# Fourier mixing and an MLP on one core: a two-element copy moved to VectorE, loads of x and y reordered, y steps placed behind the turning of u

## The chip, the cores and the metric

The kernel runs on one core of a Trainium2 chip. The metric is device time in microseconds, the median of several executions. TensorE multiplies, ScalarE, VectorE and GpSimd work elementwise, and SyncE's queue (SP in the profile) issues almost all DMAs, in order.

## The reference

Eight sequences of 3136 tokens by 256 channels in float32. Each is filtered along the tokens in the frequency domain, then mixed by a two-dimensional FFT of which the real part is added, normalized along the channels, and sent through a two-layer MLP with a ReLU and a residual:

```python
X = np.fft.rfft(x, axis=1)
y = np.fft.irfft(X * (filt_r + 1j * filt_i)[None], n=3136, axis=1).astype(np.float32)
mixed = np.real(np.fft.fft(np.fft.fft(y, axis=1), axis=2))
u = y + mixed
un = (u - u.mean(-1, keepdims=True)) / np.sqrt(u.var(-1, keepdims=True) + 1e-06)
out = u + np.maximum(un @ w_ch1, 0.0) @ w_ch2
```

## The kernel before

The transforms are matmuls with tables, in two steps each way. For every batch `forward1` and `forward2` go from x to the spectrum, multiply by the filter, keep what the mixing needs (`eo`, from `fold_sums` and `fold_halves`) and make the first inverse step, whose result goes to a DRAM scratch `d2`. `inverse2` reads pieces of `d2` (tile `b2`, 512 KB for batch 0), makes the second inverse step and writes y to DRAM (`dy`). Both are generators: `advance(n)` runs the forward one up to step n, `give(n)` the inverse one up to step n.

Tokens then go in groups of 256 pairs. A group needs its mixing (`mixture`), y read back from `dy` (`fetch`), the normalization and two products of the MLP: `first_product(g, f)` for eight slices f of the hidden channels, and `second_product(g, f)`. In the main loop `q = 8 g + f`.

Group 0 is special. Its y does not go through DRAM: `direct()` in `inverse2` sums it on TensorE into two PSUM tiles (`sums`), from near tiles and a table, in place of steps 0 and 1 of `inverse2`. `prepare_first` copies the mixing to `near` and `point` on ScalarE, spreads it to y on VectorE (lines 1078 to 1080) and GpSimd (line 1083), copies two Nyquist elements of one row (line 1086, ScalarE), adds the sums (line 1091), takes moments (1040, 1041), the root (1046, ScalarE) and five small scales (1052 to 1056, VectorE), forms u in two halves (1103, 1110, 1112) and turns it by 16 transposes on TensorE (line 327, `flip`), copied out by ScalarE and VectorE. Only then can `first_product(0, 0)` begin.

Batch 0's step c of `inverse2` for c from 2 is one matmul over half a piece (line 903), a copy by ScalarE (909) and, after every second one, four stores to `dy` (826). Piece 1 is loaded before the steps, piece 2 at step 2, piece 3 at step 4, and so on (line 821).

`warm(n, ...)` issues n matmuls whose result nobody reads, to keep TensorE's clock up. Steps 2 and 3 have six of them behind each.

Batch 1's x is seven tiles of 512 KB. `load_x(q)` loads them ahead of time, and `square_x(q)` sums their squares on ScalarE (line 480), from which comes the scale of x that batch 1's `forward1` needs (lines 518 to 530). The weights of the MLP are loaded as 64-bit words (`load_weights`, line 1255), put together by `widen_weights` on VectorE, squared for a bound and split into two halves; `take_words` only takes the buffer. `todo` is a list of such jobs with the step at which each is called (`weigh`).

The order on each engine is made by the framework's planner, which runs a model of the program and takes what it holds to be ready first; `after(key, ...)` holds an instruction behind the one that was marked with that key, where both are on the same engine's queue, and does nothing if the key is not marked yet. `marks["turn"]` is the last transpose of u, `marks["i2"]` the last matmul of `inverse2` or of the direct sums, `("bt", 6)` the last store of batch 0's `d2`, and `("y", 1)` the last load of y for group 1.

Of the kernel before, what the change touches and what calls it, by code (L numbers as in the profile page):

```python
# [9 lines left out]
F32 = mybir.dt.float32  # L10
# [216 lines left out]
def _program(ctx, tc, nc, a, NB):  # L227
# [10 lines left out]
    marks = {}  # L238
# [21 lines left out]
    def after(*keys):  # L260

        order = ExitStack()
        for k in keys:
            if k in marks:
                order.enter_context(tc.issue_after(marks[k]))
        return order
# [29 lines left out]
    idle = []  # L296
# [171 lines left out]
    def load_x(q):  # L468

        if q == len(sooner):  # L470
            take_x(q)
        with after(("bt", 6)):
            nc.sync.dma_start(sooner[q], a["x"][1, q])

    def square_x(k):
# [99 lines left out]
    def forward2(b, d1, d2):  # L575
# [223 lines left out]
        if b == 0:  # L799
# [4 lines left out]
            for _ in range(5):  # L804
                yield

    def inverse2(b, d2):
        dy = dp.tile([2, NS, 256], F32, tag="dy", name=f"dy_{b}", bufs=3)
        dys[b] = dy
        bts = {}  # L810

        def load(c):
            if c < 7:
                shape = [128, 4, 2, 256] if b else [128, 4, 256]
                bt = fp.tile(shape, F16 if b else F32, tag="b2", name=f"b2_{b}_{c}", bufs=2)
                bts[c] = bt[:112]
                with after("dy"):
                    if b:
                        move = nc.sync.dma_start(bt.rearrange("p j h c -> p (j h) c"), rows128(d2, 8 * c, 8))
                    else:  # L820
                        move = nc.sync.dma_start(bt, blocks128(d2, 4 * c, 4))
                    marks["b", c] = marks["sp"] = move.ins

        def store(k, s, r, ys, c, j0):
            rows = dy[k, 224 * c : 224 * c + 224].rearrange("(j s q) c -> s q j c", j=4, s=2)
# [24 lines left out]
                                    stop=blk == 1 and k == 1,  # L850
                                ).ins

        load(1 if b == 0 else 0)
        for _ in range(1 + WAIT):
            yield
        for c in range(14):
            if b == 0 and c < 2:
                if c == 0:
                    direct()
                yield  # L860
                continue
            if c % 2 == 0:
                load(c // 2 + 1)
                bt = bts.pop(c // 2)
                ys = fp.tile([128, 4, 256], F32, tag="ys", name=f"ys_{b}_{c}", bufs=3)
            if b:
                if c % 2 == 0:
                    yield
                    continue
                pair = []  # L870
                with nullcontext():
                    for cc in (c - 1, c):
                        o = 2 * (cc % 2)
                        p = bank(f"y_{b}_{cc}").rearrange("p (j c) -> p j c", j=2)
                        parts = [(slice(0, 1), 0), (slice(1, 2), 1)] if cc == 0 else [(slice(0, 2), 1)]
                        with after("pe" if cc == 0 else "i2"):
                            for js, t in parts:
                                for i in range(2):
                                    for h in range(2):
                                        marks["i2"] = nc.tensor.matmul(  # L880
                                            p[64 * h : 64 * h + 64, js],
                                            i2[:, t, h, i],
                                            bt[:, o + js.start : o + js.stop, h],
                                            start=i == 0,
                                            stop=i == 1,
                                        ).ins
                        pair.append((o, p))
                for o, p in pair:
                    nc.scalar.activation(ys[:, o : o + 2], p, AF.Copy, scale=alphas[b][:, 2:3])  # L889
                c //= 2  # L890
                for s in range(2):
                    store(0, s, side * s, ys, c, slice(0, 4))
                    if c:
                        store(1, s, side * (1 - s) + 28, ys, c, slice(0, 4))
                    else:
                        store(1, s, side * s + 28, ys, c, slice(0, 1))
                        store(1, s, side * (1 - s) + 28, ys, c, slice(1, 4))
                yield
                continue
            o = 2 * (c % 2)  # L900
            p = bank(f"y_{b}_{c}").rearrange("p (j c) -> p j c", j=2)
            with after("warm" if c < 4 else "turn"):
                marks["i2"] = nc.tensor.matmul(
                    p[:112], i2f[:, 1], bt[:, o : o + 2], start=True, stop=True
                ).ins
            if c < 4:
                warm(6, "i2", p=idle[0])
            with after("utt", ("cast", 0)):
                nc.scalar.copy(ys[:112, o : o + 2], p[:112])
            if o:  # L910
                c //= 2
                for s in range(2):
                    store(0, s, side * s, ys, c, slice(0, 4))
                    store(1, s, side * (1 - s) + 28, ys, c, slice(0, 4))
            yield
# [149 lines left out]
    def prepare_first():  # L1065
# [15 lines left out]
        for h, o in ((1, ALU.add), (0, ALU.subtract)):  # L1081
            with after("sum"):
                marks["sum"] = nc.gpsimd.tensor_tensor(
                    yh[row, t0, 2 + h, 1:], point[row, 0, 1:128], point[row, 0, 129:], op=o
                ).ins
        nc.scalar.copy(y[row, t0, 1, 0:129:128], point[row, 0, 0:129:128])
        yield
        ut = mp.tile([128, 2, 8, 128], F16, tag="ut", name="ut_0", bufs=2)
        mv, st, sb = small(0)
# [156 lines left out]
    def load_weights(i):  # L1246
        name = ("w1", "w2")[i // 4]
        src = a[name][:, i % 4 // 2, 512 * (i % 2) : 512 * (i % 2) + 512]
        if a[name].dtype == F32:
            words[i] = src  # L1250
            return
        if i not in words:
            take_words(i)
        with after(("bt", 6)):
            nc.sync.dma_start(words[i], src.bitcast(I32).rearrange("p (n w) -> p n w", w=2))

    def take_words(i):
# [105 lines left out]
        assert come[0] >= need(slot)  # L1363

    todo = [(n, load_weights, i) for i, n in enumerate(LOAD_AT) if n > 2]
    todo += [(57, load_x, 0), (57, load_x, 1), (61.2, load_x, 2), (61.5, load_x, 3)]
    todo += [(n, square_weights, i) for i, n in enumerate(SQUARE_AT)]
    todo += [(n, widen_weights, i) for i, n in enumerate(WIDEN_AT)]
    todo += [(n, f, w) for f, at in ((bound_weights, BOUND_AT), (split_weights, SPLIT_AT)) for n, w in zip(at, ("w1", "w2"))]
    todo.append((58.5, lower_weights, None))  # L1370
    todo += [(56.9, take_words, i) for i in (5, 6)]
    todo.sort(key=lambda t: t[0])

    def weigh(n):
# [30 lines left out]
        pass  # L1405
    first_group = prepare_first()
    next(first_group)
    for q in range(2):
        square_x(q)
    advance(59)  # L1410
    for ch in (2, 3, 6):
# [1 line left out]
    while come[0] < 1 + WAIT + 2:  # L1413
        weigh(60 + come[0])
        give(come[0] + 1)
    square_x(2)
    next(first_group)
    give(come[0] + 2)
    for _ in first_group:
        pass  # L1420
    weigh(1000)
    with after("utt"):
        nc.scalar.activation(fnyqs, fnyq, AF.Copy, scale=pF[:, 1:2])
    give(need(511))
    fetch(1)
    halves = load_halves()
    per = NS // 32
    behind = [0]
# [6 lines left out]
    for q in range(8 * ng + LAG):  # L1435
# [31 lines left out]
            next(work, None)  # L1467
        if q >= 8:
            catch_up(min(q - LAG + 1, 2 * (q - 8) + 2))
        if q in (1, 3) or q > 9:  # L1470
            give(min(come[0] + 1, soon(32 * q + SOON)))
        if q < 8:
            advance(STEPS + (0, 2, 3, 4, 5, 9, 10, 10)[q])
        else:
            advance(int(STEPS * (1 + min((q + 1) / RISE, (q + 1) / per + EARLY))))
# [63 lines left out]
```

## Time and profile before

| | us |
|---|---|
| median of 3 runs | 1434.9 |
| lowest to highest | 1434.13 to 1436.1 |
| the profiled run | 1433.79 |
| its span in the profile | 1432.0 |

| engine | busy in the span |
|---|---|
| TensorE | 97% |
| VectorE | 73% |
| ScalarE | 53% |
| GpSimd | 35% |

A view in order of time has one line for each stretch of like instructions: its start in the span and its length in us, the engine, the line of the kernel, the operation, the tiles written and read, their shapes, how many there are, and in brackets how long the engine had been idle before and what ended that. PE is TensorE, DVE VectorE, ACT ScalarE, POOL GpSimd, SPq the DMA queue of SyncE, where a line is the issue of a load or store and not its transfer. A float32 matmul of this kernel stands as two records. Everything that the change moves lies in the first 110 us.

### The profile page before, as it was taken

To read this page: it belongs to the slowest core of one execution; us is meant where nothing else is said; L and a number is where in the kernel's file an instruction comes from. 1 tells how busy PE (TensorE), PEld (TensorE's weight loads), DVE (VectorE), ACT (ScalarE), POOL (GpSimd) and SP (SyncE) were. 2 spreads that over 40 slices of the span, in tenths; PEclk is the share of its full clock that TensorE was granted. 3 is DMA by queue.
4 is the path that set the end of the run, shared out by engine and by line. 5 is a ranking of instruction groups with operands and counts; after the bars stand their busy time and mean duration, and the time that the engine had idled before them with its cause. 6 is when DMAs were issued, how large, how long until landed. Compare 5 with 4: busy or idle time off the path is not lost.

```text
span 1432.0 us, 29958 instructions
## 1 busy us (share of the span) xinstructions
PE 1387.5 (97%) x11242; PEld 946.6 (66%) x11242; DVE 1042.7 (73%) x2317; ACT 756.3 (53%) x1421; POOL 506.7 (35%) x643
## 2 busy tenths in 40 slices
PE   8869899999999999999999999999999999999998
PEld 7736576567666776667766676666766667666666
DVE  7867684788698777877588867978779876555553
ACT  6775555546465544746546554655546464434341
POOL 2501681078103930167300960047401762011010
PEclk9989999999999999999999999999999999999999
DMA  9585987699857967579766987589585977452220
GB/s 349 189 272 172 263 201 243 192 224 228 258 155 193 246 160 244 169 204 232 169 224 190 239 193 223 150 242 228 128 272 164 227 177 192 117 154 80 82 59 30
DMA packets 434350, 276.98 MB, mean 193 GB/s; under 512 B 218877, under 2 KB 400845, under 8 KB 434205
## 3 DMA queue, kind: packets, MB, share of 16 engines
q1 hardware_dynamic: 434076, 275.02, 70.0%
q8 instruction: 88, 1.44, 0.4%
q14 instruction: 58, 0.47, 0.1%
q10 hardware_dynamic: 128, 0.05, 0.0%
HBM read 124.87 MB, written 99.17 MB: 156 GB/s over the span
## 4 chain that ended last, share of the span: by engine, by line
PE 70%; DMA 11%; DVE 7%; issue 4%; ACT 3%; POOL 3%; SPq 2%; DVEq 0%; ACTq 0%; POOLq 0%
PE h L1181 27%; PE acc L1211 27%; PE y L880 3%; DMA x<-x 3%; PE s L544 2%; PE mix L982 2%; PE s L530 2%; DMA y<-dy 1%; DMA at<-d 1%; PE i L739 1%; DVE y L992 1%; PE i L741 1%; PE i L740 1%; PE s L640 1%; DVE h L1192 1%
## 5 line engine op out<-in xcount | busy, mean ns | idle before, releaser
L1211 PE MATMUL acc<-w2s,h 128*128 128x256 f16 x4704 | 596.4, 273 | 3.7 <-ACT w2s L1312 2.6
L1181 PE MATMUL h<-ut,home 128*128 128x512 f16 x2352 | 582.0, 380 | 12.4 <-DVE h L1192 7.5
L1211 PEld LDWEIGHTS <-h 128*128 128x128 f16 x4704 | 455.1, 98 | 148.2 <-issue 13.9
L1191 ACT ACTIVATE h<-h 128x512 f16<-128x512 f32 x392 | 232.7, 595 | 375.6 <-PE h L1181 370.1
L1192 DVE SCALAR_TENSOR_TENSOR h<-h,h 128x512 f16<-128x512 f32 x392 | 267.7, 685 | 211.3 <-ACT h L1191 209.4
L1181 PEld LDWEIGHTS <-home 128*128 128x128 f16 x2352 | 221.7, 98 | 223.2 <-issue 33.9
L1155 POOL TENSOR_TENSOR u<-un,u 128x512 f16<-128x512 f32 x96 | 110.4, 1166 | 620.8 <-ACT u L1154 572.3
L992 DVE SCALAR_TENSOR_TENSOR y<-mix,alpha,y 128x508 f32<-128x508 f32 (+1 forms) x360 | 152.9, 476 | 3.9 <-DMA y<-dy 2.0
L657 POOL TENSOR_TENSOR yt<-yt,t 128x224 f32<-128x224 f32 x108 | 73.0, 676 | 130.4 <-DVE t L649 80.7
L1151 ACT ACTIVATE un<-y,sb 128x256 f32<-128x256 f32 x192 | 100.0, 590 | 34.0 <-DVE sb L1056 26.8
L1220 DVE SCALAR_TENSOR_TENSOR y<-acc,beta,y 128x512 f32<-128x512 f32 x98 | 71.3, 744 | 30.3 <-PE acc L1211 30.2
L743 DVE TENSOR_TENSOR bt<-i,bt 112x512 f16<-112x512 f32 x98 | 66.2, 684 | 33.0 <-ACT bt L742 31.2
L687 POOL TENSOR_TENSOR ef<-yt 128x224 f32<-128x224 f32 x112 | 72.2, 663 | 48.7 <-DVE sb L1052 34.8
L889 ACT ACTIVATE ys<-y,alpha 128x512 f32<-128x512 f32 x98 | 64.3, 684 | 40.8 <-PE y L880 40.4
L671 POOL TENSOR_TENSOR home<-yt,home 128x448 f16<-128x448 f32 x77 | 79.3, 1035 | 13.7 <-ACT home L670 13.7
L742 ACT CAST bt<-i 112x512 f16<-112x512 f32 x98 | 56.7, 584 | 45.4 <-PE i L741 41.5
L645 DVE SCALAR_TENSOR_TENSOR yt<-s,pF,ft 128x448 f32<-128x448 f32 x98 | 65.9, 676 | 17.1 <-PE s L641 16.2
L658 POOL TENSOR_TENSOR yt<-yt,t 128x224 f32<-128x224 f32 x108 | 74.6, 693 | 0.6 <-DVE yt L651 0.6
L1040 DVE BATCH_NORM_STATS2 st<-y 128x6 f32<-128x256 f32 x196 | 73.0, 411 | 0.2
L319 DVE TENSOR_REDUCE mx<-x 112x1 f32<-112x1024 f32 x42 | 51.0, 1214 | 23.8 <-DMA x<-x 23.4
L649 DVE SCALAR_TENSOR_TENSOR t<-s,pF,ft 128x448 f32<-128x448 f32 x98 | 66.1, 675 | 0.0
L717 POOL TENSOR_TENSOR eo<-ef,eo 128x448 f16<-128x448 f32 (+6 forms) x55 | 51.5, 940 | 29.3 <-ACT eo L716 27.9
(180 smaller groups left out, 1648.1 us busy)
## 6 DMA issues: line engine op xcount, KB each, us to landing
x<-x SPq DMA_DIRECT2D x55, 512.0 KB
out<-y SPq DMA_DIRECT2D x98, 256.0 KB
at<-d SPq DMA_DIRECT2D x49, 512.0 KB
b<-d SPq DMA_DIRECT2D x49, 512.0 KB
dy<-ys SPq DMA_DIRECT2D x206, 112.0 KB
y<-dy SPq DMA_DIRECT2D x90, 256.0 KB
d<-ast SPq DMA_DIRECT2D x98, 224.0 KB
d<-bt SPq DMA_DIRECT2D x98, 224.0 KB
```

The costliest lines, as they stand in the source:

```text
L657: nc.gpsimd.tensor_tensor(yh[:, 0], yh[:, 0], t2v[:, 1], op=ALU.subtract)
L658: marks["sum"] = nc.gpsimd.tensor_tensor(yh[:, 1], yh[:, 1], t2v[:, 0], op=ALU.add).ins
L671: nc.gpsimd.tensor_tensor(ylo, ytv, yhi, op=ALU.subtract)
L687: nc.gpsimd.tensor_tensor(ef[:, i], yt[:, 0, i], yt[:, 1, i], op=o)
L992: nc.vector.scalar_tensor_tensor(out, p, al, y, op0=ALU.mult, op1=ALU.add)
L1040: nc.vector.bn_stats(st[:m, 2 * t + k], y[:m, t, k])
L1151: nc.scalar.activation(un[:m, k], y[:m, t, k], AF.Identity, bias=sb[:m, i, 1:2], scale=sb[:m, i, 3:4])
L1155: marks["u16", g] = nc.gpsimd.tensor_tensor(u16[:m, :, :, 1], unv, u16[:m, :, :, 0], op=ALU.subtract).ins
L1181: marks["pe"] = nc.tensor.matmul(p[:, c0 : c0 + n].rearrange("p (t k q) -> p t k q", k=2, q=m), homes["w1s"][:, d, hw, 128 * f : 128 * f + ...
L1191: marks["relu"] = nc.scalar.activation(h[:, 0, :nt], p[:, :nt], AF.Relu).ins
L1192: marks["h"] = nc.vector.scalar_tensor_tensor(h[:, 1, :nt], p[:, :nt], 0.0, h[:, 0, :nt], op0=ALU.max, op1=ALU.subtract).ins
L1211: nc.tensor.matmul(acc[:m, k], h[:, hh, c0 : c0 + m], w2s[:, f, hw], start=f == 0 and k == 0 and i == 0, stop=f == 7 and k == 1 and i == 2,)
```

## The change

Line 1086's copy goes from ScalarE to VectorE. The loads of pieces 1 and 2 of batch 0's y become jobs of their own (`load_piece`), called before and placed on the queue right behind the last store of `d2`; raw weights and x tiles 3 to 6 are held behind the pieces, and x tiles 5 and 6 behind group 1's last load of y too. x tiles 0 to 2 are called at step 50 instead of 57, at a time when neither key is marked, so that nothing holds them. Steps 2 and 3 of `inverse2` are held behind the transposes of u and lose their warming matmuls; twenty of these follow the direct sums instead. Steps 4 and 5 and the first `fetch` move from ahead of the main loop into its rounds 0 and 1, and steps 6 and 7 from rounds 1 and 3 to rounds 3 and 5. The third square of x is called with the first two.

```diff
--- before.py
+++ after.py
@@ -469,7 +469,7 @@
 
         if q == len(sooner):
             take_x(q)
-        with after(("bt", 6)):
+        with after("piece", ("y", 1) if q > 4 else ""):
             nc.sync.dma_start(sooner[q], a["x"][1, q])
 
     def square_x(k):
@@ -804,22 +804,34 @@
             for _ in range(5):
                 yield
 
+    pieces = {}
+
+    def load_piece(c):
+
+        bt = fp.tile([128, 4, 256], F32, tag="b2", name=f"b2_0_{c}", bufs=2)
+        with after(("bt", 6)):
+            marks["piece"] = nc.sync.dma_start(bt, blocks128(scratch[2][0], 4 * c, 4)).ins
+        pieces[c] = bt[:112]
+
     def inverse2(b, d2):
         dy = dp.tile([2, NS, 256], F32, tag="dy", name=f"dy_{b}", bufs=3)
         dys[b] = dy
         bts = {}
 
         def load(c):
-            if c < 7:
+            if c < 7 and not (b == 0 and c in pieces):
                 shape = [128, 4, 2, 256] if b else [128, 4, 256]
                 bt = fp.tile(shape, F16 if b else F32, tag="b2", name=f"b2_{b}_{c}", bufs=2)
-                bts[c] = bt[:112]
                 with after("dy"):
                     if b:
                         move = nc.sync.dma_start(bt.rearrange("p j h c -> p (j h) c"), rows128(d2, 8 * c, 8))
                     else:
                         move = nc.sync.dma_start(bt, blocks128(d2, 4 * c, 4))
                     marks["b", c] = marks["sp"] = move.ins
+                (bts if b else pieces)[c] = bt[:112]
+
+        if b == 0:
+            bts = pieces
 
         def store(k, s, r, ys, c, j0):
             rows = dy[k, 224 * c : 224 * c + 224].rearrange("(j s q) c -> s q j c", j=4, s=2)
@@ -850,7 +862,8 @@
                                     stop=blk == 1 and k == 1,
                                 ).ins
 
-        load(1 if b == 0 else 0)
+        if b:
+            load(0)
         for _ in range(1 + WAIT):
             yield
         for c in range(14):
@@ -860,7 +873,8 @@
                 yield
                 continue
             if c % 2 == 0:
-                load(c // 2 + 1)
+                if b or c > 2:
+                    load(c // 2 + 1)
                 bt = bts.pop(c // 2)
                 ys = fp.tile([128, 4, 256], F32, tag="ys", name=f"ys_{b}_{c}", bufs=3)
             if b:
@@ -899,12 +913,10 @@
                 continue
             o = 2 * (c % 2)
             p = bank(f"y_{b}_{c}").rearrange("p (j c) -> p j c", j=2)
-            with after("warm" if c < 4 else "turn"):
+            with after("turn"):
                 marks["i2"] = nc.tensor.matmul(
                     p[:112], i2f[:, 1], bt[:, o : o + 2], start=True, stop=True
                 ).ins
-            if c < 4:
-                warm(6, "i2", p=idle[0])
             with after("utt", ("cast", 0)):
                 nc.scalar.copy(ys[:112, o : o + 2], p[:112])
             if o:
@@ -1083,7 +1095,7 @@
                 marks["sum"] = nc.gpsimd.tensor_tensor(
                     yh[row, t0, 2 + h, 1:], point[row, 0, 1:128], point[row, 0, 129:], op=o
                 ).ins
-        nc.scalar.copy(y[row, t0, 1, 0:129:128], point[row, 0, 0:129:128])
+        nc.vector.tensor_copy(y[row, t0, 1, 0:129:128], point[row, 0, 0:129:128])
         yield
         ut = mp.tile([128, 2, 8, 128], F16, tag="ut", name="ut_0", bufs=2)
         mv, st, sb = small(0)
@@ -1251,7 +1263,7 @@
             return
         if i not in words:
             take_words(i)
-        with after(("bt", 6)):
+        with after("piece"):
             nc.sync.dma_start(words[i], src.bitcast(I32).rearrange("p (n w) -> p n w", w=2))
 
     def take_words(i):
@@ -1363,12 +1375,13 @@
         assert come[0] >= need(slot)
 
     todo = [(n, load_weights, i) for i, n in enumerate(LOAD_AT) if n > 2]
-    todo += [(57, load_x, 0), (57, load_x, 1), (61.2, load_x, 2), (61.5, load_x, 3)]
+    todo += [(56.95, load_piece, 1), (56.96, load_piece, 2)]
+    todo += [(49.1, load_x, 0), (49.1, load_x, 1), (49.1, load_x, 2), (61.5, load_x, 3)]
     todo += [(n, square_weights, i) for i, n in enumerate(SQUARE_AT)]
     todo += [(n, widen_weights, i) for i, n in enumerate(WIDEN_AT)]
     todo += [(n, f, w) for f, at in ((bound_weights, BOUND_AT), (split_weights, SPLIT_AT)) for n, w in zip(at, ("w1", "w2"))]
     todo.append((58.5, lower_weights, None))
-    todo += [(56.9, take_words, i) for i in (5, 6)]
+    todo += [(49, take_words, i) for i in (5, 6)]
     todo.sort(key=lambda t: t[0])
 
     def weigh(n):
@@ -1405,7 +1418,7 @@
         pass
     first_group = prepare_first()
     next(first_group)
-    for q in range(2):
+    for q in range(3):
         square_x(q)
     advance(59)
     for ch in (2, 3, 6):
@@ -1413,16 +1426,14 @@
     while come[0] < 1 + WAIT + 2:
         weigh(60 + come[0])
         give(come[0] + 1)
-    square_x(2)
     next(first_group)
-    give(come[0] + 2)
+    warm(20, "i2", p=idle[0])
     for _ in first_group:
         pass
+    give(come[0] + 2)
     weigh(1000)
     with after("utt"):
         nc.scalar.activation(fnyqs, fnyq, AF.Copy, scale=pF[:, 1:2])
-    give(need(511))
-    fetch(1)
     halves = load_halves()
     per = NS // 32
     behind = [0]
@@ -1467,8 +1478,11 @@
             next(work, None)
         if q >= 8:
             catch_up(min(q - LAG + 1, 2 * (q - 8) + 2))
-        if q in (1, 3) or q > 9:
+        if q in (0, 3, 5) or q > 9:
             give(min(come[0] + 1, soon(32 * q + SOON)))
+        if q == 1:
+            give(need(511))
+            fetch(1)
         if q < 8:
             advance(STEPS + (0, 2, 3, 4, 5, 9, 10, 10)[q])
         else:
```

## Rows read from the trace of the kernel before

**Rows 1.** the page of the profile: busy time, share of the span, instructions.

```profile
PE 1387.5 (97%) x11242; PEld 946.6 (66%) x11242; DVE 1042.7 (73%) x2317; ACT 756.3 (53%) x1421; POOL 506.7 (35%) x643
```

**Rows 2.** TensorE in order of time, 50 to 110 us.

```profile
50.94 1.94 PE L617 MATMUL s<-s2f,at 112*128 112x112 f32 x16
...
60.96 1.89 PE L294 MATMUL idle<-still 128*128 128x512 bf16 x8
...
68.82 1.89 PE L845 MATMUL y<-near,home 120*128 120x256 f32 x8
78.29 2.02 PE L903 MATMUL y<-b,i2f 112*112 112x512 f32 x2 [7.58 <-DMA b<-d_f]
...
84.86 1.06 PE L327 MATMUL utt<-ident,u 128*128 128x128 f16 x16
85.76 1.92 PE L903 MATMUL y<-b,i2f 112*112 112x512 f32 x4
87.52 2.75 PE L1181 MATMUL h<-ut,home 128*128 128x512 f16 x12
...
106.25 4.50 PE L530 MATMUL s<-x,s1f 112*112 112x512 f32 x6
```

**Rows 3.** ScalarE in order of time, 72 to 103 us.

```profile
72.63 1.06 ACT L480 ACTIVATE xsq<-x 112x1024 bf16<-112x1024 f32 x1 [5.22 <-DMA x<-x]
...
73.69 0.18 ACT L1086 COPY y<-point 1x2 f32<-1x2 f32 x1
...
77.06 0.30 ACT L1046 ACTIVATE sb<-mv,eps 128x4 f32<-128x4 f32 x1 [0.51 <-DVE mv L1041]
...
102.60 1.06 ACT L480 ACTIVATE xsq<-x 112x1024 bf16<-112x1024 f32 x1 [2.57 <-DMA x<-x]
```

**Rows 4.** VectorE in order of time, 68 to 110 us.

```profile
68.72 0.90 DVE L1080 COPY y<-near 128x8 f32<-128x8 f32 x1
73.95 0.69 DVE L1091 TENSOR_TENSOR y<-y,y 128x512 f32<-128x512 f32 x1 [4.33 <-ACT y L1086]
...
77.40 0.18 DVE L1052 RECIPROCAL sb<-sb 128x4 f32<-128x4 f32 x1 [0.37 <-ACT sb L1046]
...
78.42 1.38 DVE L1110 TENSOR_SCALAR un<-y,sb 128x256 f32<-128x256 f32 x4
79.72 1.50 DVE L1112 TENSOR_TENSOR u<-un,u 128x512 f16<-128x512 f32 x2
85.96 0.69 DVE L329 COPY ut<-utt 128x1024 f16<-128x1024 f16 x1 [4.74 <-PE utt L327]
...
109.98 0.58 DVE L1053 SCALAR_TENSOR_TENSOR sb<-sb 128x4 f32<-128x4 f32 x1
```

**Rows 5.** GpSimd in order of time, 69 to 111 us.

```profile
69.50 3.73 POOL L687 TENSOR_TENSOR ef<-yt 128x224 f32<-128x224 f32 x6
73.20 1.89 POOL L700 TENSOR_TENSOR ef<-yt 1x224 f32<-1x224 f32 x3
109.88 1.27 POOL L687 TENSOR_TENSOR ef<-yt 128x224 f32<-128x224 f32 x2 [34.79 <-DVE sb L1052]
```

**Rows 6.** SyncE's DMA queue in order of time, 52 to 96 us.

```profile
52.50 5.95 SPq L767 DMA_DIRECT2D d_f<-bt  x6
...
66.97 1.46 SPq L473 DMA_DIRECT2D x<-x  x3
...
69.82 0.57 SPq L821 DMA_DIRECT2D b<-d_f  x1
...
95.29 0.38 SPq L968 DMA_DIRECT2D y<-dy  x1
95.72 0.47 SPq L473 DMA_DIRECT2D x<-x  x1
```

**Rows 7.** the chain that ended last, 140 to 170 us: start, us, what.

```profile
142.91 0.88 PE y L903 x2
...
160.26 5.11 DMA ut<-u
```

## The prediction

> **What bounds the kernel now.** I read the page first: TensorE is busy 97% of the span [rows 1]. Only time in which it does no useful work can be won, and only where no later wait takes it back. TensorE's order of time comes next [rows 2]: the direct sums of group 0 end at 68.82 + 1.89 = 70.71, the first product of group 0 begins at 87.52, and solid work begins at 106.25. In the row at 78.29 the reader is to see a wait of 7.58 us for the first piece of y. But the piece is not all that is late there: the turning of u (line 327) is at 84.86, behind two y steps and twelve warming matmuls.
>
> Why is u late? In ScalarE's order [rows 3] the first square of x begins at 72.63, after 5.22 us of waiting for its load, and the two-element copy of line 1086 stands behind it, at 73.69. VectorE [rows 4] is done with line 1080 at 69.62 and idles 4.33 us for that copy. So the load of x, which nothing of group 0 needs, delays group 0. The u tiles are done at 79.72 + 1.50 = 81.22, and TensorE turns them 3.64 us later.
>
> **The copy moved to VectorE.** On ScalarE it takes 0.18 us [rows 3]. On VectorE it follows line 1080 at 69.62. That row is itself a small copy (8 elements a partition), and it took 0.90 us [rows 4]; GpSimd runs six folds from 69.50, 3.73 / 6 = 0.62 us each [rows 5]. The bounds are 0.18 and 0.90; I take 0.6, one fold's time, as that is what runs beside it. The first of the direct sums is ready by then, so line 1091 begins at 70.2 instead of 73.95.
>
> From there the path is priced by its own rows. Line 1091 to the root on ScalarE takes 77.06 - 73.95 = 3.11, so the root is at 73.3. ScalarE is free for it if x has landed: it idles from 72.63 - 5.22 = 67.41, and the three squares and the copy, with the root's own wait, fill at most 77.06 - 72.63 = 4.43 us, which ends at 71.8. Root to reciprocal is 0.34, so the small scales begin at 73.65. The five of them took 78.42 - 77.40 = 1.02, about 0.2 each, after GpSimd had ended (73.20 + 1.89 = 75.09). Now they meet it. Beside a GpSimd fold that began at 109.88, such a step took 0.58 at 109.98 [rows 4, 5]. So the five cost between 1.02 and 2.5; I take 1.8, since some two or three of them fall before 75.09. They end at 75.4 instead of 78.42: of 3.75 us won, 0.75 is lost here.
>
> This is where a rule speaks against the change. The Trainium skill (SBUF — State Buffer, "Who interferes with whom") says that VectorE and GpSimd share a pair of ports, that a VectorE copy in a two-port mode, or an instruction of two SBUF inputs beside a GpSimd instruction that reads SBUF, contends for it, and that the second to issue waits until the first is done. By that rule alone the sum would go by the upper ends above, with 1 us less won. The rows of 0.90 and 0.58 agree with it; the 0.69 us of line 1091 at 73.95 beside GpSimd, with one input in PSUM, does not speak against it [rows 4, 5].
>
> From the end of the scales to the end of u is 81.22 - 78.42 = 2.80, so u is done at 78.2, 3.0 us sooner.
>
> **The y steps behind the turning of u.** The turning loses the two y steps and twelve warming matmuls ahead of it, which ran at the lower clock at first (2.02 us for a step at 78.29, 1.92 for two at 85.76) [rows 2]. So its second half comes at 78.2; it ends at 78.7, and VectorE's copy of 0.69 (the row at 85.96) is ready at 79.4 [rows 4]. The y steps 2 and 3, 1.8 us together, fill 78.7 to 80.5. The first product begins at 80.5 instead of 87.52: **7.0 us sooner**. But steps 4 and 5, which stood ahead of the product, now come after it, 1.8 us of TensorE work that is only put off. **Net 5.2.**
>
> The twenty warming matmuls cost nothing if they fit: eight took 1.89 at 60.96 [rows 2], so twenty take 4.7 and end at 75.4, ahead of 78.2, which is their cover. At twice that they would end at 80.2 and the product would be some 2 us later. They follow the direct sums at once, so I take the first.
>
> **The pieces and x on the load queue.** Today three loads of x are issued from 66.97, and the first piece at 69.82 lands 8.5 us later, by 78.29 [rows 2, 6]. In the change the pieces come right behind the last stores of d2, and raw weights and later x behind them. Even at the old landing time step 2 (78.7) would not wait; with three tiles of 512 KB less ahead of it I expect it sooner. The three x loads carry no mark. Buffers come free for them as the spectra are done, the last of which ends at 50.94 + 1.94 = 52.88 [rows 2], and as the inverse steps behind them are done. If they are issued before 62, ScalarE's squares do not wait. If the queue puts them ahead of the stores that begin at 52.50 [rows 6], the stores are held until 52.9 or, for the last tile, an inverse step or two more: 0 to some 2 us on the direct sums. I take 0, as VectorE has other work up to 69.62 that the sums do not set.
>
> **What is late next.** x tiles 5 and 6 are now held behind the second load of y for group 1, at present at 95.29 [rows 6]. Step 5 ended at 85.76 + 1.92 = 87.68; its copy, its stores and their landing took 7.6 from there, a part of it ScalarE's other work. In the change step 5 ends after one or two products, at about 85; with 6.3 for the rest the y load is at 91.3 and the last x at 92.1. That landing took 102.60 - 95.72 = 6.9 [rows 3, 6]; with tile 5 beside it up to 1.5 more, and one or two squares of 1.06 follow. The last square thus ends between 100.1 and 102.6 instead of 103.7: 1.1 to 3.6 us sooner. The weights w2 start from VectorE's copy of ut, 7 us sooner, but go through the same engines. TensorE's solid stretch from 106.25 therefore moves by **1 to 7 us**. Between the middle of the x path (2.4), TensorE's own work (5.2) and w2 (7) I take **4.5**, since w2's products can run before the scale of x.
>
> The wait for ut at 160.26 (5.11 us) stands on a chain that goes back to TensorE's own y steps at 142.91 [rows 7], so it should move along with them.
>
> **Sum.** 1432.0 - 4.5 = 1427.5 of span and 1429.3 for the profiled run, which lies 1.8 above its span. The median lies 1.1 above that run: 1434.9 - 4.5 = **1430.4**.
>
> **Rivals.**
> 1. *More is won.* w2's products begin before the scale of x, and fill its gap: 7 or 8 us, 1427.5. For it: w2 starts 7 us sooner. Against: x's scale goes through VectorE in the same stretch. 0.11.
> 2. *x is not early*: its loads get no buffer, or wait behind the stores and pieces. The first square is at 72.63 as today; without gaps the root is some 0.4 sooner, the order's 3.64 is won, and 1.8 put off: 1432.7. For it: buffers free only from 52.88. Against: no mark holds them. 0.14.
> 3. *Given back later.* The ut of a later group comes when the DMA engines have moved it, whatever TensorE does, and the wait at 160.26 grows by what was won: 1434.9. For it: 5.11 us of landing there. Against: the chain before it. 0.14.
> 4. *Slower*: x 5 and 6 behind y. The point from which it decides is the second y load at about 93: then the last x is at 94, lands at 102.4 with both tiles' time, and two squares end at 104.5, past today's 103.7. If step 5 is put behind three or four products instead of one or two, and its stores behind other loads, the y load comes at 96 to 97 and the solid stretch begins some 3.5 us later than today: 1438.4. Against: the product itself is 7 us sooner. 0.12.
> The forecast keeps 0.49.
>
> **How the numbers follow.** 0.2% is 2.9 us, about what a measurement of this kernel can tell from no change. Faster (below 1432.0): the forecast, rival 1 and a little of rival 2, together 0.61. Same: the rest of rival 2 and rival 3, 0.27. Slower: 0.12. The range, 1426.0 to 1437.0, takes in rivals 1 to 3 and the bounds of the copy, the scales, the warming and the x path, and leaves out rival 4.
>
> **What would show it.** Right: line 1091 at about 70; the scales ending near 75.4, some of them near 0.6 us; line 327 near 78, ahead of step 2; the first product near 80.5; warming matmuls of about 0.24 us; solid work from about 102. Wrong: squares of x that still wait for loads after 70; the second y load of group 1 after 93 and the last square after 104; a wait for ut near 160 that has grown by what was won.

## The result and the profile after

The changed kernel takes 1448.45 us in the median (1444.78 to 1451.96), the kernel before beside it 1434.55. The ratio is 1.0094, with a 95% interval of 1.0074 to 1.0113: **slower by 14 us, where 4.5 us less was forecast.** The profiled run took 1447.88, its span is 1446.1. Most lines of the changed kernel from 826 on stand 12 further down (845 is 857, 1091 is 1103, 1181 is 1193, 1211 is 1223); 903 is 917.

TensorE in order of time, 71 to 118 us, which answers to [rows 2]:

```profile
71.59 3.75 PE L857 MATMUL y<-near,direct 120*128 120x256 f32 x8 [4.87 <-DMA near<-bt]
75.14 2.81 PE L857 MATMUL y<-near,home 120*128 120x256 f32 x8
77.78 4.48 PE L294 MATMUL idle<-still 128*128 128x512 bf16 x20
82.10 0.22 PE L327 MATMUL utt<-ident,u 128*128 128x128 f16 x1
...
84.39 2.78 PE L917 MATMUL y<-b,i2f 112*112 112x512 f32 x6
87.01 2.75 PE L1193 MATMUL h<-ut,home 128*128 128x512 f16 x12
...
108.13 0.59 PE L1223 MATMUL acc<-w2s,h 128*128 128x256 f16 x2 [7.12 <-ACT w2s L1324]
108.92 5.04 PE L1223 MATMUL acc<-w2s,h 128*128 128x256 f16 x35 [0.20 <-DVE w2s L1311]
113.79 0.21 PE L312 MATMUL pb_x<-lines_x,still 112*128 112x112 bf16 x1
...
117.67 1.88 PE L530 MATMUL s<-x,s1f 112*112 112x512 f32 x4
```

Three things are new. The direct sums wait 4.87 us for the near tiles and end at 77.95 instead of 70.71. The first product begins at 87.01, only 0.51 us sooner than before. And the products with w2 now stand ahead of the scale of x (`pb_x`), after a wait of 7.12, so batch 1's first matmuls (line 530) begin at 117.67 instead of 106.25. Before, only the first of these products stood ahead of it:

```profile
105.47 0.38 PE L1211 MATMUL acc<-w2s,h 128*128 128x256 f16 x2 [2.61 <-ACT w2s L1312]
106.15 0.21 PE L312 MATMUL pb_x<-lines_x,still 112*128 112x112 bf16 x1 [0.30 <-DVE lines_x L307]
```

SyncE's queue from 52 to 100 us, which answers to [rows 6]:

```profile
52.23 4.54 SPq L767 DMA_DIRECT2D d_f<-bt  x5
56.83 1.91 SPq L473 DMA_DIRECT2D x<-x  x3
58.86 0.35 SPq L767 DMA_DIRECT2D d_f<-bt  x1
66.25 1.41 SPq L754 DMA_DIRECT2D near<-d_f  x2
67.71 3.17 SPq L760 DMA_DIRECT2D near<-bt  x4
...
97.04 0.38 SPq L980 DMA_DIRECT2D y<-dy  x1
...
99.11 0.43 SPq L473 DMA_DIRECT2D x<-x  x1
```

Three tiles of x, 1.5 MB, are issued ahead of the last 224 KB store that the near loads read back. The near load (line 754) is issued at 66.25, 7.0 us behind the end of that store's row; before it was issued at 61.35, 2.9 us behind the same store.

VectorE (first three lines) and ScalarE (last four) in order of time, which answer to [rows 4] and [rows 3]:

```profile
69.18 0.51 DVE L1098 COPY y<-point 1x2 f32<-1x2 f32 x1
75.44 0.69 DVE L1103 TENSOR_TENSOR y<-y,y 128x512 f32<-128x512 f32 x1 [5.75 <-PE y L857]
80.26 0.17 DVE L1065 SCALAR_TENSOR_TENSOR sb<-sb 128x4 f32<-128x4 f32 x1
66.77 1.04 ACT L480 ACTIVATE xsq<-x 112x1024 bf16<-112x1024 f32 x1
79.71 0.30 ACT L1058 ACTIVATE sb<-mv,eps 128x4 f32<-128x4 f32 x1 [9.73 <-DVE mv L1053]
104.49 1.06 ACT L480 ACTIVATE xsq<-x 112x1024 bf16<-112x1024 f32 x1 [4.20 <-DMA x<-x]
106.32 1.06 ACT L480 ACTIVATE xsq<-x 112x1024 bf16<-112x1024 f32 x1 [0.20 <-DMA x<-x]
```

The copy and the early squares do what they should (the copy ends at 69.69, the squares begin at 66.77 without a wait). Then VectorE waits 5.75 us for TensorE's sums. Late in the head, ScalarE waits 4.20 us for x tile 5 and the last square ends at 107.4 instead of 103.7; the scaling of w2 stands behind it on the same engine.

**Where the 14 us went.** The end of a group shows on VectorE as the addition of line 1220 (1232 after). Group 0's and group 6's in the changed kernel:

```profile
122.42 0.75 DVE L1232 SCALAR_TENSOR_TENSOR y<-acc,beta,y 128x512 f32<-128x512 f32 x1 [1.35 <-PE acc L1223]
...
339.46 1.40 DVE L1232 SCALAR_TENSOR_TENSOR y<-acc,beta,y 128x512 f32<-128x512 f32 x2
```

Before, the same two begin at 120.39 and 325.06. So the head costs only 2.0 us, and another 12.4 are lost between groups 0 and 6. By group 8 the lag is 11.9, at group 15 it is 12.0, at the end 14.1. Below, "lag" is this difference to the kernel before. A lag compares one profile with one profile; the profile of before took 1433.79 us, 1.6 to 3 less than the medians of before beside the experiments, so a lag of 2 or 3 us at the end says little.

TensorE's busy time from 120 to 345 us, before and then after (columns: stretch, its length, busy time and matmuls, granted clock as a share of full speed, share of the DMA engines, GB/s):

```profile
120.00:345.00 225.00, 214.26 (x1818) 0.98 0.84 224
```

```profile
120.00:345.00 225.00, 206.94 (x1720) 0.98 0.84 219
```

TensorE idles 18.1 us there instead of 10.7. The waits of TensorE in that stretch of the changed kernel (engine, tile and line, releaser: us in total, times, longest):

```profile
PE i L739 <- DMA z<-y: 6.2, 3, 3.5
...
PE s L640 <- DMA at<-d: 2.3, 2, 1.8
```

These are batch 1's transforms, which go through DRAM between their steps (`at`, `z`): begun 11 us later, they come late by turns. The orders of instructions, aligned engine by engine, show the same: VectorE, ScalarE, GpSimd and SyncE differ between the two kernels only up to some 375 us (VectorE in one instruction more, at 453), and are alike from there on. So the change moves work far behind the first 110 us. In that stretch the planner has two orders. In one, batch 1's x scale and its first matmuls stand ahead of the products of w2 (before). In the other they stand behind (after).

### The profile page after: what moved, and what is told of

It reads as the page before. It is cut to its first block, busy times and chain, and to the rows that moved or that the text cites. A ratio compares the mean times of both kernels' runs of the same rounds, so it can differ in the third digit from the quotient of the medians.

```text
span 1446.1 us, 29982 instructions
## 1 busy us (share of the span) xinstructions
PE 1392.1 (96%) x11250; PEld 949.9 (66%) x11250; DVE 1047.9 (72%) x2318; ACT 755.4 (52%) x1420; POOL 506.3 (35%) x643
## 4 chain that ended last, share of the span: by engine, by line
PE 65%; DMA 12%; DVE 8%; issue 5%; POOL 4%; ACT 4%; SPq 3%; DVEq 0%; ACTq 0%; POOLq 0%
PE h L1193 25%; PE acc L1223 25%; DMA x<-x 3%; PE s L544 2%; PE y L894 2%; PE mix L994 2%; DMA at<-d 2%; DMA d<-ast 2%; DVE y L1004 2%; DVE h L1204 1%; PE i L739 1%; PE i L741 1%; PE i L740 1%; PE s L640 1%; PE s L530 1%
## 5 line engine op out<-in xcount | busy, mean ns | idle before, releaser
L739 PE MATMUL i<-z,i 112*112 112x256 f16 x196 | 54.4, 277 | 9.2 <-DMA z<-y 6.2
```

## The experiments

Three suspects: the loads of x ahead of the last store of d2; x tiles 5 and 6 held behind the second y load; and the order of x's scale and w2. In the expectations, theory A has the loss as a sum of separate parts, and B has what is lost after 120 us as a mere consequence of the late start; C puts it on the order of x's scale and w2, and D on the late start or the moved loads. Ratios are to the kernel before, run beside each. The median of before was 1436.8 us beside the first four experiments, 1436.6 beside the next four, 1435.4 beside the last four.

**The copy alone**, on the kernel before:

```diff
-        nc.scalar.copy(y[row, t0, 1, 0:129:128], point[row, 0, 0:129:128])
+        nc.vector.tensor_copy(y[row, t0, 1, 0:129:128], point[row, 0, 0:129:128])
```

> The kernel before with the two-element copy on VectorE and nothing else. Both theories: line 1091 at about 70.2 instead of 73.95. But the root on ScalarE stands behind three squares of x, which end at about 76.5, so it moves by 0.5 us at most, and the first y step waits for its piece until 78.3 as before. So 1434.5, within 1.5 us of the kernel before: the copy by itself is worth nothing as long as x and the piece come late. If instead the turning of u comes over 1 us sooner, the wait for x on ScalarE was not the bound.

Measured: 1436.04, ratio 1.0001 (0.9985 to 1.0017). VectorE, and then ScalarE:

```profile
69.50 0.50 DVE L1086 COPY y<-point 1x2 f32<-1x2 f32 x1
...
76.58 0.18 DVE L1052 RECIPROCAL sb<-sb 128x4 f32<-128x4 f32 x1 [3.31 <-ACT sb L1046]
72.50 1.06 ACT L480 ACTIVATE xsq<-x 112x1024 bf16<-112x1024 f32 x1 [5.32 <-DMA x<-x]
```

The copy ends at 70.00 and lets VectorE go on 3.8 us sooner (line 1091 begins at 70.13), and 3.31 of it comes back as a wait for the root, which stands behind the squares on ScalarE. Without earlier x loads the copy brings the small scales 0.8 us sooner, and the turning, behind its y steps, 0.35. The lag at group 0 is -1.5 and at group 15 -0.2.

**x tiles 5 and 6 not held**, on the changed kernel:

```diff
-        with after("piece", ("y", 1) if q > 4 else ""):
+        with after("piece"):
```

> The changed kernel without the hold of x tiles 5 and 6 behind group 1's second load of y. Theory A (the loss is a sum of separate parts: the early x loads, the late x 5 and 6, and an order of the later steps that is worse by itself): ScalarE's wait of 4.2 us for x tile 5 goes, w2's scaling starts some 2 to 3 us sooner than 107.4, and the time falls by 2 to 3 us, to about 1446. Theory B (what is lost after 120 us is only a consequence of the late start): the time falls by more, 5 us or over, to 1443 or less. If the time doesn't move, ScalarE's wait was covered by something else.

Measured: 1451.29, ratio 1.0108 (1.0091 to 1.0126); nothing won. Tile 5 comes sooner, but tile 6 is still issued behind a y load, at 99.59, and its square waits 5.61 us and begins at 106.00. So freeing the hold alone does not bring the last tile sooner, and what the hold costs is not shown by this run.

**x tiles 0 to 2 behind the near loads from DRAM** (`far` marks the last of them), on the changed kernel:

```diff
-        with after("piece", ("y", 1) if q > 4 else ""):
+        with after("far" if q < 3 else "piece", ("y", 1) if q > 4 else ""):
...
-    todo += [(49.1, load_x, 0), (49.1, load_x, 1), (49.1, load_x, 2), (61.5, load_x, 3)]
+    todo += [(55.5, load_x, 0), (55.5, load_x, 1), (55.5, load_x, 2), (61.5, load_x, 3)]
```

> The changed kernel with x tiles 0 to 2 called later, so that they stand on the queue behind the last stores of d2 and ahead of the pieces, as in the kernel before. Both theories: the wait of 4.9 us for the near tiles goes and the direct sums end at 70.7 instead of 77.8; but the squares of x wait for x again, the root is at about 76.5, and u is turned at about 80, 3 us sooner than 83.1. Theory A: some 3 to 4 us less than the changed kernel, 1444.5. Theory B: near the kernel before, 1436 or less.

Measured: 1449.72, ratio 1.0092 (1.0067 to 1.0117). SyncE, and then TensorE:

```profile
60.51 1.41 SPq L754 DMA_DIRECT2D near<-d_f  x2
...
67.95 1.89 PE L857 MATMUL y<-near,home 120*128 120x256 f32 x8
```

The wait for the near tiles is gone, the sums end 8.1 us sooner than in the changed kernel and the first product begins at 84.29. The lag at group 0 falls from 2.0 to -0.2, yet it is 13.9 at group 6 and 15.9 at the end. So the price of the early loads at the head is shown, and it is not where the 14 us are: neither theory's time came (1444.5 or 1436).

**Both edits together:**

```diff
-        with after("piece", ("y", 1) if q > 4 else ""):
+        with after("far" if q < 3 else "piece"):
...
```

> Both edits of the two runs above: x tiles 0 to 2 behind the stores, tiles 5 and 6 not held behind y. Theory A: the two gains add, 1442, and still 7 us over the kernel before, with group 0 ending near 118 and the lag growing between groups 0 and 8. Theory B: 1434 or less, as group 0 then ends sooner than in the kernel before (120.4).

Measured: 1445.53, ratio 1.0072 (1.0043 to 1.0101): 3 us better than the changed kernel, though the two intervals overlap, and still 9 us slower than before. Its last x tile is squared from 103.28. More than half of the loss is left with both load suspects gone.

**The turning alone**: y steps 2 and 3 behind it, warming moved, on the kernel before (copy and loads as before):

```diff
-            with after("warm" if c < 4 else "turn"):
+            with after("turn"):
...
-            if c < 4:
-                warm(6, "i2", p=idle[0])
...
-    give(come[0] + 2)
+    warm(20, "i2", p=idle[0])
     for _ in first_group:
         pass
+    give(come[0] + 2)
```

> The kernel before with the y steps 2 and 3 behind the turning of u, and the warming matmuls moved, and no other part of the change. The copy stays on ScalarE, so u comes no sooner, but the turning stands ahead of the two y steps: u turned some 3 us sooner than 84.86. Theory C: the planner then puts batch 1's x scale behind w2, so group 0 ends 1 to 3 us sooner and yet the lag grows behind it: 1440 to 1445. Theory D: 1432 to 1434, faster than the kernel before.

Measured: 1444.9, ratio 1.007 (1.0047 to 1.0093). TensorE:

```profile
79.07 0.29 PE L327 MATMUL utt<-ident,u 128*128 128x128 f16 x1 [4.42 <-ACT u L1101]
...
82.02 5.26 PE L903 MATMUL y<-b,i2f 112*112 112x512 f32 x8
...
114.95 1.88 PE L530 MATMUL s<-x,s1f 112*112 112x512 f32 x4
```

u is turned from 79.07 instead of 84.86, and the first product still begins at 87.12: all four y steps stand between them. But this part alone puts batch 1's first matmuls behind w2 (114.95), and the lag goes from -0.7 at group 0 to 7.2 at group 6 and 12.4 at the end, as theory C had it. No load of x or y was reordered by hand here.

**The other order alone**, on the kernel before: one edge that holds the lines of x's scale behind the last scaling of w2:

```diff
-        marks["lines", name] = nc.vector.tensor_scalar(
-            lines, ident[:rows, :rows], col, 1e-18, op0=ALU.mult, op1=ALU.max
-        ).ins
+        with after("w2l" if name == "x1" else ""):
+            marks["lines", name] = nc.vector.tensor_scalar(
+                lines, ident[:rows, :rows], col, 1e-18, op0=ALU.mult, op1=ALU.max
+            ).ins
```

> The kernel before with one ordering edge: the spread of batch 1's x scale (pow2, line 307) is held behind VectorE's last part of the w2 scaling. Nothing else of the change is in it. Theory C (what was lost after 120 us comes from the place of batch 1's x scale behind the w2 scaling, which puts batch 1's first matmuls some 10 us later in TensorE's order and with it all of batch 1's forward transform): group 0 ends at or before 120.4, batch 1's first matmuls at line 530 come at 115 or later instead of 106.3, and from there the lag grows to 8 to 12 us at group 8: 1443 to 1446. Theory D (it comes from the late start of group 0 or from the moved loads): within 2 us of the kernel before.

Measured: 1442.1, ratio 1.0042 (1.0019 to 1.0066). TensorE in order of time:

```profile
113.19 0.22 PE L313 MATMUL pb_x<-lines_x,still 112*128 112x112 bf16 x1
...
116.63 1.88 PE L531 MATMUL s<-x,s1f 112*112 112x512 f32 x4
```

With everything else as before, this one edge costs 5.5 us. The lag is 1.0 at group 0, 7.4 at group 6 and 4.9 at group 8 (8 to 12 were expected there), and TensorE idles 15.7 us from 120 to 345 us. Behind 131 us its order is that of the changed kernel on VectorE, ScalarE, GpSimd and SyncE. So the order by itself costs. Whether it costs because batch 1's transforms begin 10 us later, or because the long stretch is then interleaved otherwise, was not separated: this edge brings both.

**Before's order on the changed kernel**, by holding w2's scaling behind x's scale:

```diff
-            with after("spread", "fold", "relu"):
+            with after("spread", "fold", "relu", ("xroot", 1) if name == "w2" else ""):
...
-            lowered[:] = [nc.vector.scalar_tensor_tensor(lo, w, scale, hi, op0=ALU.mult, op1=ALU.subtract).ins]
+            with after(("lines", "x1")):
+                lowered[:] = [nc.vector.scalar_tensor_tensor(lo, w, scale, hi, op0=ALU.mult, op1=ALU.subtract).ins]
...
-        if q == 5:
+        if q == 7:
```

> The changed kernel with the opposite edge: the w2 scaling is called two rounds later and held behind batch 1's x scale on ScalarE and VectorE, so that batch 1's first matmuls stand ahead of the w2 products again, as in the kernel before. Theory C: group 0 ends later than in the changed kernel (124 to 126, since w2 now waits for x tile 6), but the lag doesn't grow: at group 8 it is at most what it was at group 0, 1438 to 1441. Theory D: the lag grows as in the changed kernel, 1448 or more.

Measured: 1443.44, ratio 1.0054 (1.0033 to 1.0075): 5.0 us better than the changed kernel, and less good than C expected. The lag is 2.8 at group 0, 3.1 at group 6 and at group 8: the loss between groups 0 and 6 is gone (idle 10.5 us in that stretch). What is left is the head's, and a later step.

**The same on the version with both load edits:**

```diff
-        with after("piece", ("y", 1) if q > 4 else ""):
+        with after("far" if q < 3 else "piece"):
...
-            with after("spread", "fold", "relu"):
+            with after("spread", "fold", "relu", ("xroot", 1) if name == "w2" else ""):
...
```

> The same edge, with x tiles 0 to 2 back behind the stores of d2 and tiles 5 and 6 no longer held behind y. Theory C: group 0 ends between 118 and 121 and the lag stays there: 1432 to 1436, the kernel before or a little under it. Theory D: as with both those edits alone, 1442 to 1446.

Measured: 1440.91, ratio 1.0033 (1.0016 to 1.0051), 4.6 us better than without the edges. In its profile the lag is -0.2 at groups 0 to 2 and 0.6 at group 15, then 4.8 at group 21 and at the end. The time lies between what C and D expected. The engines' orders are those of before from the head on, so this later step is not the order's; TensorE there waits for tiles from DRAM (line 640, 2.42 us at about 620 us, 0.34 before). TensorE at the end of the head:

```profile
104.85 0.58 PE L1223 MATMUL acc<-w2s,h 128*128 128x256 f16 x2 [6.38 <-ACT w2s L1325]
...
105.39 5.12 PE L530 MATMUL s<-x,s1f 112*112 112x512 f32 x6
```

**The edges alone, and the parts under them.** Four more kernels on the one before, all with these edges: nothing else; the turning; the turning and the copy; the piece loads ahead of the raw words and all x tiles.

```diff
+            with after("spread", "fold", "relu", ("xroot", 1) if name == "w2" else ""):
...
```

> The kernel before with nothing but the two edges of the earlier runs that hold the w2 products behind batch 1's x scale; the order of the long stretch stays that of before. A control. If the order alone carries the loss (theory C): 1436.6 us, ratio 0.999 to 1.001, group 0 and the last group within 1.5 us of before. If these edges have a price of their own, which would be in the two earlier runs that used them (they came out 4.5 and 7 us above before): 1439 to 1441, lost from the x scale at 105 on.

```diff
+            with after("turn"):
...
+    warm(20, "i2", p=idle[0])
...
```

> The kernel before with the y steps 2 and 3 behind the turning of u and the warming matmuls moved, copy still on ScalarE, and with the x scale held ahead of the w2 products. Theory C: the turning alone cost 8.3 us, of which 5 to 5.5 were the flipped order, so 1439 to 1440. The prediction's step (an earlier first product is worth about 5 net): 1431 to 1432. That turning sooner is worth nothing and costs nothing once the order is kept: 1436.6.

```diff
+        nc.vector.tensor_copy(y[row, t0, 1, 0:129:128], point[row, 0, 0:129:128])
...
+            with after("turn"):
...
+    warm(20, "i2", p=idle[0])
...
```

> As the run before it, with the two-element copy on VectorE besides: all parts of the change but the loads. The prediction's sum: 1430 to 1431. Theory C, with what is won at the head waiting for w2 and x again: 1436 to 1438, and the first product at 82 to 84. If moved y steps cost by themselves: 1440, as in the version with the loads kept off the stores.

```diff
+        with after("piece"):
             nc.sync.dma_start(sooner[q], a["x"][1, q])
...
+        with after("piece"):
             nc.sync.dma_start(words[i], src.bitcast(I32).rearrange("p (n w) -> p n w", w=2))
...
+    todo += [(56.95, load_piece, 1), (56.96, load_piece, 2)]
```

> The kernel before with only the loads of the pieces put first (x tiles and raw words held behind them), and the x scale held ahead of the w2 products. Theory C: 1436 to 1438. If the order of loads carries what is left of the loss: 1440 or more, with the last tile of x landing after 104 and the x scale's wait longer than 2 us.

| kernel | us | ratio, interval | lag at group 0, 8, end |
|---|---|---|---|
| edges alone | 1438.32 | 1.0020 (1.0001 to 1.0039) | 1.3, 0.0, 4.3 |
| turning | 1437.43 | 1.0016 (0.9998 to 1.0035) | -0.2, -2.2, 3.9 |
| turning and copy | 1434.85 | 1.0005 (0.9987 to 1.0022) | 0.9, 1.1, 5.6 |
| pieces first | 1435.39 | 1.0003 (0.9989 to 1.0017) | -2.4, -3.9, -0.4 |

The turning that cost 8.3 us with the order flipped costs 2 with it kept, which the measurement cannot tell from nothing. The edges alone came out a little above what C expected, inside neither of its two cases. The last three cannot be told from before. TensorE of the kernel with turning and copy, and of the one with the pieces first:

```profile
80.46 0.29 PE L327 MATMUL utt<-ident,u 128*128 128x128 f16 x1 [3.54 <-ACT u L1101]
...
83.39 5.46 PE L903 MATMUL y<-b,i2f 112*112 112x512 f32 x8
88.68 4.05 PE L1179 MATMUL h<-ut,home 128*128 128x512 f16 x18
...
106.19 0.59 PE L1209 MATMUL acc<-w2s,h 128*128 128x256 f16 x2 [4.37 <-ACT w2s L1311]
...
106.85 4.83 PE L530 MATMUL s<-x,s1f 112*112 112x512 f32 x6
```

```profile
103.84 4.55 PE L530 MATMUL s<-x,s1f 112*112 112x512 f32 x6
```

With turning and copy, u is turned 4.4 us sooner, but all four y steps stand behind it and the first product begins at 88.68, 1.2 us later than before; the solid stretch begins at 106.85, behind a wait of 4.37 us for w2's scaling. Where the first product did come sooner, the time turned into that wait: with both load edits and before's order it comes 3.05 us sooner (84.47), the wait grows from 2.61 to 6.38, and line 530 begins 0.9 us sooner (105.39). It moves most with the pieces first, where x's last tile comes sooner too (103.84, x 6 issued at 90.70). No version here beats the kernel before by more than the measurement can tell.

**All fourteen programs side by side.** From 131 us on, VectorE, ScalarE, GpSimd and SyncE have one of only two orders. The changed kernel and five of the others have the new one (x 5 and 6 not held, x 0 to 2 behind the near loads, both, the turning alone, the other order alone); their lag grows by 3.7 to 11.6 us between groups 0 and 8. The other seven have that of before; their lag changes by -2.0 to 0.9. So the growth comes with the new order and with nothing else that was tried. How large it is under that order, from 3.7 with both load edits to 9.9 in the changed kernel and 11.6 with x tiles 0 to 2 behind the near loads, is set by something that these runs do not show.

## Why the prediction was wrong, point by point

**The step that failed is "What is late next".** It looked for the next late thing among transfers and engines, and took the order of the work behind the head as fixed. The order is the planner's, and the turning alone already moves it: it pushes batch 1's x scale behind w2. That is worth 4.6 to 5.5 us by three comparisons (the edge on before, and the edges on the changed kernel with and without the load edits), and 7.5 by the two versions with the turning; by the intervals each is good to 3 to 5 us. No rival held it. The prediction even took w2 ahead of x's scale for the way in which the gap is filled; with that order batch 1's transforms begin 10 us later, and TensorE's waits of the next 200 us are mostly for them.

The same step fails with the order kept. It took 4.5 us for the move of the solid stretch, more than x's path alone gave (2.4). With before's order and both load edits the stretch begins 0.9 us sooner: x's scale and w2's scaling both stand behind the last square of x on ScalarE, and that square ends 0.7 us sooner (102.97 against 103.66).

**The early x loads were priced at 0, with 2 as the upper end.** They cost 4.87 us of waiting and 2.8 us of lower clock, 7.2 us at the end of the sums. The prediction named the place (three loads ahead of the stores) but counted only the wait for their buffers, not what 1.5 MB in the queue do to the store behind it. At the head that took back nearly all that u had won: first product at 87.01, not 80.5. The move of these loads behind the near loads took 2.2 us off the lag at group 0; in the whole time, with the hold on x 5 and 6 taken away too, it gave 3 us in the median, not clear of noise.

**Rival 4 came about at its own point**: second y load at 97.04, past 93, last square ending at 107.4, past 104.5. The start of solid work, 3.5 us late by its sum, was 1.9 late (108.13 against 106.25). It had a chance of 0.12; since piece loads, y steps and first fetch were all put back, it deserved more. But it is the smaller part: with hold and early loads both in and before's order, the lag is 2.8 at group 0 and 3.1 at group 8.

**"Steps 2 and 3 fill 78.7 to 80.5, steps 4 and 5 come after."** Three steps stood ahead of the product in the changed kernel (84.39, 6 records), four with the turning alone, in part at the lower clock (0.50 from 82 to 84 us). So of the 3.64 us that stood ahead of the turning, 2.8 came back behind it.

**What held.** The copy took 0.51 us where 0.6 was taken. The squares no longer waited after 70, and the turning came ahead of step 2. Twenty warming matmuls took 4.48 (4.7) and fitted. The five scales were priced at 1.8 for GpSimd beside them and took 0.17 or so each, since GpSimd had ended at 74.54 when they came at 80. The rule of the Trainium skill (SBUF — State Buffer, "Who interferes with whom"), by which the second of two contending instructions waits for the first, was therefore not tried at that place; it was at another, where four of the same scales for the next group met folds from 111.63 on. VectorE, and then GpSimd:

```profile
111.80 0.51 DVE L1065 SCALAR_TENSOR_TENSOR sb<-sb 128x4 f32<-128x4 f32 x1
112.34 0.58 DVE L1066 SCALAR_TENSOR_TENSOR sb<-mv,sb 128x4 f32<-128x4 f32 x1
112.96 0.17 DVE L1067 SCALAR_TENSOR_TENSOR sb<-sb 128x4 f32<-128x4 f32 x1
111.63 1.27 POOL L687 TENSOR_TENSOR ef<-yt 128x224 f32<-128x224 f32 x2 [37.09 <-DVE eo L722]
112.98 0.66 POOL L700 TENSOR_TENSOR ef<-yt 1x224 f32<-1x224 f32 x1
```

The trace agrees with the rule there: 0.51 and 0.58 beside a fold, 0.17 for the step that began between two of GpSimd's instructions, ahead of the second.

**Rival 3** (given back at the wait for ut near 160) is not seen as such: in the changed kernel that wait is gone, as the order is another one; with the order of before TensorE waits there 4.6 to 5.2 us in seven versions, against 4.9 in the kernel before, whatever was won at the head.

**What stays open.** With order, early loads and hold all taken back, the loss falls from 13.9 us to 4.3, each against the kernel before beside it: some 9 of the 14 us. That version, with all other parts, is still some 4 us above before, while turning and copy, or pieces, under the same order are within 1. A part of the 4 may be the price of the edges, which alone came out 2.9 us above before (0.1 to 5.6). In its profile 4.2 us of that come between groups 15 and 21, with the orders alike. The edges alone lose 3.7 us between groups 15 and 35, and the version with the pieces first gives back 3.1 there. Behind group 15 every profile, that of the copy alone too, loses 1.5 to 6.3 us against the one profile of before. Whether that step belongs to these programs or varies from execution to execution (one version's profiled run took 1439.43, its median is 1434.85) was not settled.

## What to carry to other kernels

Where a planner makes the order, compare the two programs' orders on each engine before pricing any wait: moving a few matmuls at the head reordered some 300 us of work behind it, and that cost more than the waits that the move was to remove. A load that nobody needs soon should not be issued ahead of a store that somebody reads back. And before an early stage is sped up, name the last input of the next solid stretch (here x's last tile and w2's scaling); if it does not move, the time won turns into a wait for it.

## What the runs showed of the hardware

In this kernel, loads delayed the store behind them for about as long as their bytes take. The stretch of 58 to 62 us, before and then after, all engines (columns: stretch, length, busy time of TensorE, its weight loads, VectorE, ScalarE, GpSimd, then clock, DMA share, GB/s):

```profile
58.00:62.00 4.00, 3.07 (x14) 1.92 (x14) 4.00 (x18) 2.47 (x6) 0.00 (x0) 1.00 0.36 121
```

```profile
58.00:62.00 4.00, 3.39 (x16) 2.11 (x16) 3.82 (x18) 2.47 (x6) 0.00 (x0) 1.00 0.89 273
```

At 273 GB/s, 1.5 MB take 5.8 us; the dependent load was issued 4.9 us later than before. The Trainium skill (DMA: Bandwidth & Descriptors, "Queues, rings and completion order") states that each DMA engine takes the descriptors of a queue's ring in order; these 4.9 us fit that, though the trace does not show the order on each engine.

TensorE's clock fell with the waits, to the lower of its two levels (1.2 GHz). The changed kernel, TensorE alone (columns: stretch, length, busy time and matmuls, clock as a share of full speed, DMA share, GB/s):

```profile
71.50:73.50 2.00, 1.91 (x5) 0.50 0.73 234
...
108.10:110.00 1.90, 1.67 (x8) 0.50 0.84 281
...
112.00:114.00 2.00, 2.00 (x21) 1.00 0.00 0
```

After the wait of 4.87 us the granted clock is 0.50, and eight matmul records of the direct sums take 3.75 us where 1.89 is their time at full clock; after the one of 7.12 it is 0.50 again, and full from 112 on. So this wait at the head cost more than its length: 2.8 us on top of 4.87.
